# A Fourier mixer and its feed-forward block on one core: the inverse step of the next token group moved into another unit, with store, split and weight-sum steps rescheduled

## The chip, the cores and the metric

The kernel runs on one core of a Trainium2 chip. The metric is the device time of one execution in microseconds; the change is judged by the median of several runs. A core has TensorE (PE; its weight loads are PEld), VectorE (DVE), ScalarE (ACT), GpSimd (POOL) and SyncE (SP), which here only issues DMAs. Each engine works through its own queue in order.

## The reference, cut to what matters

```python
X = np.fft.rfft(x, axis=1)                     # x: (8, 3008, 256)
Y = X * (filt_r + 1j * filt_i)[None]
y = np.fft.irfft(Y, n=3008, axis=1).reshape(8 * 3008, 256)
h = y @ w_in                                   # (24064, 256) @ (256, 2048)
g = h - np.tanh(h)
out = g @ w_out                                # (24064, 2048) @ (2048, 256)
```

Eight sequences of 3008 tokens are filtered in the frequency domain and then go through two matrix products with `h - tanh(h)` between them. All is float32.

## The kernel before, in words

**Work.** 3008 = 64 x 47, so the transform is made in steps: a 64-point step on the input (`first` for batches 1 and 2, `split_first` for batches 3 to 7, a program of its own for batch 0), written to a DRAM buffer `ct1`; a 47-point step, the filter and the 47-point step back (`middle`), from `ct1` to a DRAM buffer `ct2`; and an inverse 64-point step (`last`), from `ct2` to on-chip tiles `ut` and `tu`, which are the input of the first matrix product. Tokens are treated in 48 groups: 8 batches `p` of 6 groups `c`.

**Units.** For each group the feed-forward block runs in four units `u`, each a quarter of the 2048 inner columns. Unit `U = 4 * group + u`. In the loop over `U`, three units overlap: the first product of unit U (`up`), the nonlinearity of U - 1 (`shrink`), the second product of U - 2 (`down`). Both products take seven block products for eight, with sums of blocks (`combine` for the data, `sums` for the weights). So a unit has 7 + 7 block products of two 128x128 by 128x256 pieces each; each piece shows as two matmuls in the trace, 56 in a unit. The first group, whose weight sums are not there yet, uses plain products (`up_plain`, `down_plain`).

**Slots.** `up` is written out by hand. Between its products it calls `d` and `e` (the next piece of `down`), `s` (the next piece of `shrink`) and five slots `t(0)` to `t(4)`. A slot first puts up to four entries of the list `outs` on SyncE's queue (`store_some(4)`), in slot 2 makes the output tile of the group before and adds its 32 (or 48) stores to `outs` (`store`), and then runs at most one piece of side work: the inverse step of the next group at (u, k) = (3, 2); a piece of `first`; a piece of `split_first` at the places `SPLIT_AT`, each (c, u, k); or a piece of `middle` (a plan of `there`, eight filter pieces and `back`, four times a batch; `there` stands at (2, 0)). Side work puts its writes to `ct1` and `ct2` at the front of `outs`.

**Order on the engines.** The order in which the program calls these is the order on each engine's queue. In `up`, bank `x` takes product 1, then in turn 6, 7 and 4 on top, with ScalarE (`s1`, `u2`, `u3`, L629) or VectorE (L671) reading it between; bank `y` takes product 2 (read by L646); bank `z` takes product 5 (L663), then 3 on top (L679). The accumulators of `down` are the banks `o0` to `o3`; `o3` is read last, by L834. Bank `t` is left over for side work, which borrows others when they are free.

**Side work.** `last` (L582) makes two banks with 64x64 matmuls; ScalarE copies one out (L586), VectorE adds and subtracts the other (L589, L590), GpSimd makes the four sums `tu` (L603 to L606). `packed` (L402) makes the 47-point steps with 24x32 matmuls in four banks. `split_first` (L341) makes the 64-point step with 32x32 matmuls in four banks, in three parts a batch: load of `f` (L314) and of two x tiles (L321, L325, L327), their sum (L332) and difference (L334), matmuls and copies (L346, L347), sums and differences (L349, L350) and writes to `ct1`. At unit 3 of a batch's last group the loop begins `split_first` of batch p + 3, whose first loads are issued there, and `middle` of batch p + 2 (loads of `a2`, L375, and `ft`, L383). The sum L332 stands in slot (0, 0, 2) of the next batch.

Of the kernel before, what the change touches and what calls it, by code (L numbers as in the profile page):

```python
# [9 lines left out]
F32 = mybir.dt.float32  # L10
# [7 lines left out]
BATCH, SEQ, DM = 8, 3008, 256  # L18
# [6 lines left out]
CH = 4  # L25
# [92 lines left out]
def kernel(  # L118
# [104 lines left out]

        return jobs

    def sums(u):

        w = (wu if u < 4 else wd)[:, :, 256 * (u % 4):256 * (u % 4) + 256]
        V.tensor_add(w[:, 4], w[:, 6], w[:, 3])
        yield  # L230
        for to, one_in, less in ((5, 4, 0), (2, 1, 5), (6, 0, 6)):
            V.tensor_sub(w[:, to], w[:, one_in], w[:, less])
            yield

    def begun(tiles, job, queue=nc.sync):
        j = converted(tiles, *job, queue)
# [70 lines left out]
    def split_first(b, z):  # L307

        quarters = [slice(32 * k, 32 * k + 32) for k in range(4)]
        for c, tags in enumerate((("t", "o1", "y", "o0"), ("t", "o3", "o1", "o2"),  # L310
                                  ("t", "o1", "y", "o0"))):
            f = tr.tile([128, XH, 128], F32, tag="f", bufs=2, name="f")[:, 0:2]
            f = f.rearrange("p a (b n) -> p (a b) n", n=32)
            nc.sync.dma_start(f, split_d[:, 256 * c:256 * c + 256])  # L314
            x0, x1 = (tr.tile([128, XH, DM], F32, tag="x", bufs=2, name="x_sb") for _ in range(2))
            for h, t in enumerate((x0, x1)):
                at = b * SEQ + 32 * h * NR
                for g in range(2):
                    r = 2 * FH * c + FH * g
                    low, high = quarters[g], quarters[2 + g]  # L320
                    nc.sync.dma_start(t[low], dram(x.tensor, (at + r) * DM,  # L321
                                                   [[NR * DM, 32], [1, FH * DM]]))
                    lo = int(r == 0)
                    if lo:
                        nc.sync.dma_start(t[high, 0], dram(x.tensor, at * DM,  # L325
                                                           [[NR * DM, 32], [1, DM]]))
                    nc.sync.dma_start(t[high, lo:FH], dram(x.tensor, (at + NR - r - lo) * DM,  # L327
                                                           [[NR * DM, 32], [-DM, FH - lo], [1, DM]]))
            yield
            both = tr.tile([128, 2, 2, DM], F32, tag="a1", bufs=1, name="a1")  # L330
            even = both.rearrange("p v n c -> p (v n) c")
            V.tensor_add(even, x0, x1)  # L332
            yield
            V.tensor_sub(x1, x0, x1)  # L334
            yield
            banks = z(tags)
            for n in range(2):
                for k, (bank, part) in enumerate(zip(banks, quarters)):
                    for j, to in enumerate(quarters):
                        m, odd = 2 * (j // 2) + n, j % 2  # L340
                        nc.tensor.matmul(bank[to, n], f[part, 2 * m + odd],  # L341
                                         (x1 if odd else even)[part, m], start=True, stop=True)
            made = both, x0.rearrange("p (v n) c -> p v n c", v=2)
            other = x1[:, 0:2]
            for g, a1 in enumerate(made):
                ACT.copy(a1[:, 1], banks[2 + g])  # L346
            ACT.copy(other, banks[1])  # L347
            for g, a1 in enumerate(made):
                V.tensor_add(a1[:, 0], other if g else banks[0], a1[:, 1])  # L349
                V.tensor_sub(a1[:, 1], other if g else banks[0], a1[:, 1])  # L350
                outs[:0] = [(dram(ct1[b], ((1 - j % 2) * NH + 2 * FH * c + FH * g +
                                           2 * (j // 2)) * DM,
                                  [[2 * NH * DM, 32], [64 * NH * DM, 2], [1, 2 * DM]]),
                             a1[part].rearrange("p v n c -> p v (n c)"))
                            for j, part in enumerate(quarters)]
                yield

    SPLIT_AT = {(0, 0, 2), (0, 1, 0), (0, 1, 3), (1, 1, 1), (1, 1, 4), (2, 0, 2),
                (3, 0, 2), (4, 2, 0), (4, 2, 2), (4, 3, 0), (5, 0, 2), (5, 1, 0), (5, 1, 3),
                (5, 2, 2)}  # L360

    def parts(t, b, g, first_block=0, n=4, step=1):

# [24 lines left out]
    def packed(banks, o, weight, data):  # L388

        ahead, whole, late = [], [], []  # L390
        for q, bank in enumerate(banks):
            part = slice(PAD * q, PAD * q + NH)
            for col in range(4):
                to, at = bank[PAD * col:PAD * col + PAD], data(q, col)[part]
                plain, special = (wide[part, weight(q, col, last)] for last in (0, 1))
                if o == 3 and 3 == (col if weight is WAYS[0] else q):
                    ahead.append((to[:, 0], plain, at[:, 0:DM]))
                    late.append((to[:, 1], special, at[:, DM:2 * DM]))
                else:
                    whole.append((to.rearrange("p n c -> p (n c)"), plain, at))  # L400
        for to, weights_of, at in ahead + whole + late:
            nc.tensor.matmul(to, weights_of, at, start=True, stop=True)  # L402
# [165 lines left out]

    e2s, uts = {}, {}

    def last(i, z):

        b, c = groups[i]
        n = sum(widths(c))
# [3 lines left out]
        for h in range(2):  # L578
            for j, r in enumerate(order(c)):
                for bank, half in zip(banks, rows):  # L580
                    for m, part in enumerate(rows):
                        nc.tensor.matmul(bank[part, h, j],  # L582
                                         e2[half, r - CH * c, h * 128 + 64 * m:h * 128 + 64 * m + 64],
                                         gt[half, r - CH * c], start=True, stop=True)
        odd = tr.tile([128, 2, CH, 64], F32, tag="e1", bufs=2, name="odd")
        ACT.copy(odd, banks[1])  # L586
        u4 = ut.rearrange("p h (j n) -> p h j n", n=128)
        m = sum(w == 128 for w in widths(c))
        V.tensor_add(u4[:, :, :, 0:64], banks[0], odd)  # L589
        V.tensor_sub(u4[:, :, 0:m, 127:63:-1], banks[0][:, :, 0:m], odd[:, :, 0:m])  # L590
        w = n // 2
        if i == 0:
            uts[i] = (ut, None, w)
# [13 lines left out]

    hs, gs = {}, {}

    def up(U, d, e, s, t):  # L610

        i, u = divmod(U, 4)
        b, tu, w = uts[i]
        rhs = [b[0][0], b[1][0], b[1][1], tu[:, 3, 0:w], tu[:, 0, 0:w], tu[:, 1, 0:w],
               tu[:, 2, 0:w]]
# [24 lines left out]
        mm(X, 1, True)  # L640
        mm(Y, 2, True)
        s1 = copied("s1")
        t(0)
        d()
        shrinks(0)
        V.tensor_add(h[:, 0, :, 0:w], Y, s1)  # L646
# [359 lines left out]
    with tc.tile_pool(name="tr", bufs=2) as tr, tc.manual_schedule():  # L1006
# [278 lines left out]
        with tc.tile_pool(name="dn", bufs=2) as dn, \  # L1285
# [5 lines left out]
            def zd2(name, shape):  # L1291
                return [ps.tile(shape, F32, tag=tag, bufs=1, name=name) for tag in "ty"]

            def zd4(tags):
                return [ps.tile([128, 2, DM], F32, tag=tag, bufs=1, name="pm") for tag in tags]

# [55 lines left out]
            kinds.update({at: "filter" for at in FILTERED})  # L1352

            firsts, mids = {2: fs}, {}
            for U in range(total + 2):
                i, u = divmod(U, 4)
                if U == 6:
                    assert not pending
                    late = (None for u in (3, 5, 6, 7) for _ in sums(u))
                if U == 3:  # L1360
                    G.dma_start(mats[:, 0:10 * PAD], wide_d[0:KM])
                if U < total:
                    p, c = groups[i]
                    if c == 0 and u == 0 and 0 < p < BATCH - 1:
                        plan += STAGES
                    if u == 0 and i + 1 < len(groups) and c + 1 < NC:
                        e2s[i + 1] = load_e2(*groups[i + 1])
                    if u == 2 and i + 1 < len(groups) and c + 1 == NC:
                        assert not plan
                        e2s[i + 1] = load_e2(*groups[i + 1])  # L1370
                    if u == 3 and c + 1 == NC and p + 3 < BATCH:
                        firsts[p + 3] = split_first(p + 3, zd4)
                        next(firsts[p + 3])
                    if u == 3 and c + 1 == NC and p + 2 < BATCH:
                        mids[p + 2] = middle(p + 2, zd4)
                        next(mids[p + 2])
# [15 lines left out]
                def e():  # L1392

                    next(dw, None)
                    converting((U < 6) * (3 if U > 1 else 1))

                def s():

# [2 lines left out]
                def t(k):  # L1401
# [7 lines left out]
                    if i == 1 and pos == LEAD - 7:  # L1409
# [1 line left out]
                        mids[1] = middle(1, zd4)  # L1411
                        next(mids[1])
                        plan.extend(STAGES)
                    if (u, k) == (3, 2) and i + 1 < len(groups):
                        next(last(i + 1, z2))
                    elif due and due[0] <= pos and (U < 4 or u < 3 and k == 2):
                        due.pop(0)
                        next(firsts[2])
                    elif (c, u, k) in SPLIT_AT and 0 < p < BATCH - 2:
                        next(firsts[p + 2])  # L1420
                    elif plan and plan[0] == kinds.get((u, k)):
                        plan.pop(0)
                        next(mids[p + 1])
# [58 lines left out]
```

## Time and profile before

| | |
|---|---|
| median of three runs | 2556.81 us (2555.12 to 2558.86) |
| the profiled execution's own time | 2556.91 us |
| span of its trace | 2555.1 us |
| TensorE, weight loads | 2534.3 us, 2169.1 us busy |
| VectorE, ScalarE, GpSimd | 1873.3 us, 1667.7 us, 1481.2 us busy |

The span is the time from the first to the last instruction in the trace. Busy time is the time in which an engine had at least one instruction under way; issuing a DMA does not count. Rows of the timeline give start, duration (of all instructions that the row merges), engine, line, and `out<-in` with shapes; the count is at the end, and in brackets the idle time of the engine before it with what ended it.

### The profile page before, as it was taken

The numbers are of one execution on the slowest core, as the hardware profiler recorded it, in microseconds if no ns is written. First come the engines' busy times: TensorE is split into PE (matmuls) and PEld (weight loads), VectorE is DVE, ScalarE is ACT, GpSimd is POOL, SyncE is SP. The second block draws the span as 40 slices with busy tenths as digits, with TensorE's granted clock in tenths as the row PEclk, the third lists the DMA queues.
The fourth block names the chain that finished last, engine by engine and source line by source line (L and its number), as shares of the span: only waits on it lengthen the run. The fifth ranks groups of instructions, "written<-read, shape, count | busy, mean of one in ns | idle before, by whom it ended". The sixth has DMA issues, their size and how long they took to land.

```text
span 2555.1 us, 44617 instructions
## 1 busy us (share of the span) xinstructions
PE 2534.3 (99%) x17072; PEld 2169.1 (85%) x17072; DVE 1873.3 (73%) x2262; ACT 1667.7 (65%) x2499; POOL 1481.2 (58%) x1120
## 2 busy tenths in 40 slices
PE   9999999999999999999999999999999999999998
PEld 8578889888898888988888888888889888898887
DVE  6887776887678876888668886688866877555555
ACT  4556666666666666666666666666666666666665
POOL 5266665666466665666556665566645666555552
PEclk9999999999999999999999999999999999999999
DMA  8863224422343323342233322443123322110110
GB/s 247 263 173 103 65 53 109 102 65 61 81 104 91 81 59 98 80 110 58 73 95 98 84 65 61 107 101 97 36 67 85 93 66 51 26 32 18 25 22 19
DMA packets 334240, 212.42 MB, mean 83 GB/s; under 512 B 231709, under 2 KB 305595, under 8 KB 330369
## 3 DMA queue, kind: packets, MB, share of 16 engines
q1 hardware_dynamic: 319667, 185.98, 29.6%
q0 software_dynamic: 11120, 16.16, 2.4%
q10 hardware_dynamic: 3230, 7.34, 0.8%
q8 instruction: 136, 2.23, 0.4%
q14 instruction: 87, 0.71, 0.1%
HBM read 128.86 MB, written 83.39 MB: 83 GB/s over the span
## 4 chain that ended last, share of the span: by engine, by line
PE 94%; DVE 2%; DMA 2%; issue 0%; ACT 0%; POOL 0%; SPq 0%; ACTq 0%; POOLq 0%; DVEq 0%
PE o L795 44%; PE x L623 25%; PE z L623 12%; PE y L623 6%; PE pm L402 3%; PE pu L582 2%; PE pm L341 1%; DMA ct<-a 1%; DMA x<-in_x_dram 1%; DMA filt<-in_filt_r_dram 0%; DMA ct<-e 0%; DVE h L745 0%; PE pf L298 0%; PE o L857 0%; PE pe L1115 0%
## 5 line engine op out<-in xcount | busy, mean ns | idle before, releaser
L795 PE MATMUL o<-t,wd 128*128 128x256 f32 (+1 forms) x3008 | 763.2, 376 | 0.0
L603 POOL TENSOR_TENSOR t<-h 128x512 f32<-128x512 f32 (+1 forms) x186 | 305.5, 1643 | 712.6 <-DVE h L745 696.0
L745 DVE TENSOR_TENSOR h<-h,y 128x1024 f32<-128x1024 f32 (+1 forms) x384 | 579.3, 1509 | 161.9 <-ACT y L741 158.5
L795 PEld LDWEIGHTS o<-t,wd 128*128 128x128 f32 x3008 | 568.3, 190 | 86.3 <-POOL o L827 15.1
L623 PE MATMUL x<-tu,wu 128*128 128x256 f32 (+1 forms) x2256 | 576.0, 378 | 0.6 <-ACT u L629 0.6
L795 PE MATMUL o<-h,wd 128*128 128x256 f32 (+1 forms) x2256 | 573.2, 377 | 0.2 <-DVE h L745 0.2
L795 PEld LDWEIGHTS o<-h,wd 128*128 128x128 f32 x2256 | 425.3, 190 | 71.7 <-issue 18.4
L629 ACT COPY s<-x 128x512 f32<-128x512 f32 (+1 forms) x188 | 108.8, 578 | 564.9 <-PE x L623 564.5
L623 PEld LDWEIGHTS x<-tu,wu 128*128 128x128 f32 x2256 | 422.9, 190 | 58.3 <-issue 3.7
L738 ACT ACTIVATE y<-y 128x1024 f32<-128x1024 f32 (+1 forms) x384 | 399.4, 1040 | 12.0
L741 ACT ACTIVATE y<-y 128x1024 f32<-128x1024 f32 (+1 forms) x384 | 399.8, 1041 | 4.6
L735 ACT ACTIVATE y<-h 128x1024 f32<-128x1024 f32 (+1 forms) x384 | 400.5, 1043 | 2.5 <-DVE h L671 1.7
L604 POOL TENSOR_TENSOR t<-h,t 128x512 f32<-128x512 f32 (+1 forms) x186 | 314.0, 1688 | 14.6
L606 POOL TENSOR_TENSOR t<-h,t 128x512 f32<-128x512 f32 (+1 forms) x186 | 304.6, 1638 | 0.0
L605 POOL TENSOR_TENSOR t<-h 128x512 f32<-128x512 f32 (+1 forms) x186 | 289.8, 1558 | 0.0
L629 ACT COPY u<-x 128x512 f32<-128x512 f32 (+1 forms) x376 | 213.6, 568 | 56.8 <-PE x L623 53.6
L671 DVE COPY h<-x 128x512 f32<-128x512 f32 (+1 forms) x188 | 127.7, 679 | 127.1 <-PE x L623 127.0
L623 PE MATMUL z<-tu,wu 128*128 128x256 f32 (+1 forms) x752 | 190.1, 375 | 0.4 <-DVE h L679 0.4
L623 PE MATMUL z<-ut,wu 128*128 128x256 f32 (+1 forms) x752 | 190.1, 375 | 0.4 <-DVE h L663 0.4
L623 PE MATMUL x<-ut,wu 128*128 128x256 f32 (+1 forms) x752 | 190.1, 375 | 0.2 <-DVE h L671 0.2
L623 PE MATMUL y<-ut,wu 128*128 128x256 f32 (+1 forms) x752 | 190.1, 375 | 0.2 <-ACT a L300 0.2
L663 DVE TENSOR_TENSOR h<-z,u 128x512 f32<-128x512 f32 (+1 forms) x188 | 127.1, 676 | 73.0 <-ACT u L629 72.1
(211 smaller groups left out, 2798.1 us busy)
## 6 DMA issues: line engine op xcount, KB each, us to landing
ft<-filt SPq DMA_DIRECT2D x28, 1024.0 KB
ct<-nn SPq DMA_DIRECT2D x56, 512.0 KB
e<-ct SPq DMA_DIRECT2D x47, 512.0 KB
a<-ct SPq DMA_DIRECT2D x112, 192.0 KB
out_dram<-ot SPq DMA_DIRECT2D x1248, 16.0 KB
x_sb<-in_x_dram SPq DMA_DIRECT2D x110, 128.0 KB
ct<-a SPq DMA_DIRECT2D x60, 128.0 KB
ct<-x_sb SPq DMA_DIRECT2D x60, 128.0 KB
```

The source lines that it names most:

```text
L603: by.tensor_sub(t[0], b[0][1], b[0][0])
L604: by.tensor_sub(t[1], b[1][1], t[0])
L605: by.tensor_sub(t[2], b[1][1], b[0][1])
L606: by.tensor_sub(t[3], b[1][0], t[1])
L623: nc.tensor.matmul(bank[:, k], wu[:, q - 1, (2 * u + k) * 128:(2 * u + k + 1) * 128], rhs[q - 1], start=(first and k == 0), stop=True, ski ...
L629: ACT.copy(t, X)
L671: V.tensor_copy(h[:, 2, :, 0:w], X)
L735: ACT.activation(y[k], ht[k], AF.Arctan, scale=TURN)
L738: ACT.activation(y[k], y[k], AF.Tanh, scale=BEND)
L741: ACT.activation(y[k], y[k], AF.Square, scale=SCALE, accum_out=y_sums[:, 2 * U + k // 2:2 * U + k // 2 + 1])
L745: V.tensor_mul(ht[k], ht[k], y[k])
L795: nc.tensor.matmul(product(q), wd[:, q - 1, (2 * u + k) * 128: (2 * u + k + 1) * 128], rhs[q - 1][:, k], start=(u == 0 and k == 0 and q == ...
```

## The change

- `last` of the next group moves from slot (3, 2) to slot (2, 0) in the groups for which `merged` holds: those where `there` or a split part stands in that slot. It then uses banks `y` and `x`, and ScalarE copies both out (`held`). In these units `up` calls slot 0 ahead of its first product instead of behind its second. The load of `e2` in a batch's last group moves from unit 2 to unit 0.
- `packed` takes its four banks in the order 0, 2, 3, 1 on the way there.
- `split_first`: ScalarE copies all four banks instead of three, each of the four sums and differences gets a slot, and the parts use other banks; `SPLIT_AT` has 23 places instead of 14. The third part's matmuls move from (5, 1, 3) to (5, 2, 0), its last difference from (5, 2, 2) to (5, 2, 4).
- At unit 3 of a batch's last group, all of `outs` is put on SyncE's queue before the loads of `split_first` and `middle`.
- Of the weight sums of four quarters, which ran two a slot from unit 6, the first three of each run in unit 5 (three at each `e`), and the last of each in unit 6.

```diff
-    def sums(u):
+    def sums(u, n=4):
 
         w = (wu if u < 4 else wd)[:, :, 256 * (u % 4):256 * (u % 4) + 256]
         V.tensor_add(w[:, 4], w[:, 6], w[:, 3])
         yield
-        for to, one_in, less in ((5, 4, 0), (2, 1, 5), (6, 0, 6)):
+        for to, one_in, less in ((5, 4, 0), (2, 1, 5), (6, 0, 6))[:n - 1]:
             V.tensor_sub(w[:, to], w[:, one_in], w[:, less])
             yield
+
+    def last_sum(u):
+
+        w = (wu if u < 4 else wd)[:, :, 256 * (u % 4):256 * (u % 4) + 256]
+        V.tensor_sub(w[:, 6], w[:, 0], w[:, 6])
...
-        for c, tags in enumerate((("t", "o1", "y", "o0"), ("t", "o3", "o1", "o2"),
-                                  ("t", "o1", "y", "o0"))):
+        for c, tags in enumerate((("t", "y", "o1", "o0"), ("t", "o3", "o1", "o2"),
+                                  ("t", "o3", "o1", "o2"))):
...
-            other = x1[:, 0:2]
+            others = x1.rearrange("p (v n) c -> p v n c", v=2)
+            for k in (1, 0, 2, 3):
+                ACT.copy(made[k - 2][:, 1] if k > 1 else others[:, k], banks[k])
+            yield
             for g, a1 in enumerate(made):
-                ACT.copy(a1[:, 1], banks[2 + g])
-            ACT.copy(other, banks[1])
-            for g, a1 in enumerate(made):
-                V.tensor_add(a1[:, 0], other if g else banks[0], a1[:, 1])
-                V.tensor_sub(a1[:, 1], other if g else banks[0], a1[:, 1])
+                V.tensor_add(a1[:, 0], others[:, g], a1[:, 1])
+                yield
+                V.tensor_sub(a1[:, 1], others[:, g], a1[:, 1])
...
-    SPLIT_AT = {(0, 0, 2), (0, 1, 0), (0, 1, 3), (1, 1, 1), (1, 1, 4), (2, 0, 2),
-                (3, 0, 2), (4, 2, 0), (4, 2, 2), (4, 3, 0), (5, 0, 2), (5, 1, 0), (5, 1, 3),
-                (5, 2, 2)}
+    SPLIT_AT = {(0, 0, 2), (0, 1, 0), (0, 1, 3), (1, 0, 1), (1, 0, 2), (1, 1, 1), (1, 1, 2),
+                (1, 1, 4), (2, 0, 2), (3, 0, 2), (4, 2, 0), (4, 2, 1), (4, 2, 2), (4, 2, 3),
+                (4, 2, 4), (4, 3, 0), (5, 0, 2), (5, 1, 0), (5, 2, 0), (5, 2, 1), (5, 2, 2),
+                (5, 2, 3), (5, 2, 4)}
...
-        for q, bank in enumerate(banks):
+        for q in (0, 2, 3, 1) if weight is WAYS[0] else range(4):
+            bank = banks[q]
...
-        odd = tr.tile([128, 2, CH, 64], F32, tag="e1", bufs=2, name="odd")
-        ACT.copy(odd, banks[1])
+        even, odd = banks
+        for k in (1, 0) if held else (1,):
+            t = tr.tile([128, 2, CH, 64], F32, tag="e1", bufs=2, name=("even", "odd")[k])
+            ACT.copy(t, banks[k])
+            even, odd = (even, t) if k else (t, odd)
...
-        V.tensor_add(u4[:, :, :, 0:64], banks[0], odd)
-        V.tensor_sub(u4[:, :, 0:m, 127:63:-1], banks[0][:, :, 0:m], odd[:, :, 0:m])
+        V.tensor_add(u4[:, :, :, 0:64], even, odd)
+        V.tensor_sub(u4[:, :, 0:m, 127:63:-1], even[:, :, 0:m], odd[:, :, 0:m])
...
+    def merged(U):
+
+        i, u = divmod(U, 4)
+        b, c = groups[i]
+        return u == 2 and (1 < c < NC - 1 if b == 0 else
+                           c < (4 if b == BATCH - 2 else NC) and b < BATCH - 1)
+
     def up(U, d, e, s, t):
 
         i, u = divmod(U, 4)
+        if merged(U):
+            t(0)
...
         s1 = copied("s1")
-        t(0)
+        if not merged(U):
+            t(0)
...
+            def z2u(name, shape):
+                return [ps.tile(shape, F32, tag=tag, bufs=1, name=name) for tag in "yx"]
...
+            extra = (None for u in (3, 5, 6, 7) for _ in sums(u, 3))
...
-                    late = (None for u in (3, 5, 6, 7) for _ in sums(u))
+                    for _ in extra:
+                        pass
+                    late = (last_sum(u) for u in (3, 5, 6, 7))
...
-                    if u == 0 and i + 1 < len(groups) and c + 1 < NC:
+                    at = (2, 0) if merged(4 * i + 2) else (3, 2)
+                    if i + 1 < len(groups) and u == (2 if (p, c) == (0, NC - 1) else 0):
+                        assert c + 1 < NC or not plan
                         e2s[i + 1] = load_e2(*groups[i + 1])
-                    if u == 2 and i + 1 < len(groups) and c + 1 == NC:
-                        assert not plan
-                        e2s[i + 1] = load_e2(*groups[i + 1])
+                    if u == 3 and c + 1 == NC:
+                        store_some(len(outs))
...
+                    if U == 5:
+                        assert not pending
+                        for _ in range(3):
+                            next(extra, None)
...
-                    if (u, k) == (3, 2) and i + 1 < len(groups):
-                        next(last(i + 1, z2))
+                    behind = i + 1 < len(groups) and (u, k) == at
+                    if behind:
+                        next(last(i + 1, z2 if u == 3 else z2u, u == 2))
+                    if behind and u == 3:
+                        pass
                     elif due and due[0] <= pos and (U < 4 or u < 3 and k == 2):
```

More of the change, by code (lines that the diff above doesn't have):

```diff
@@ L569, with last @@
     e2s, uts = {}, {}
-    def last(i, z):
+    def last(i, z, held=False):
         b, c = groups[i]
```

## Prediction

> **What bounds the kernel now.** I read the page first (busy times and the chain that ended last), then the groups of TensorE instructions with shapes kept apart, and then the timeline around the places that the diff touches.
>
> ```profile
> span 2555.1 us, 44617 instructions
> PE 2534.3 (99%) x17072; PEld 2169.1 (85%) x17072; DVE 1873.3 (73%) x2262; ACT 1667.7 (65%) x2499; POOL 1481.2 (58%) x1120
> PE 94%; DVE 2%; DMA 2%; issue 0%; ACT 0%; POOL 0%; SPq 0%; ACTq 0%; POOLq 0%; DVEq 0%
> ```
>
> TensorE is busy for 2534.3 of 2555.1 us, and 94% of the chain is its own. The diff takes no matmul away, so it can win only the 21 us of idle time and whatever is lost between matmuls; against that, every microsecond for which it makes TensorE wait counts in full. I therefore look at the distance between starts of matmuls.
>
> ```profile
> L795 PE MATMUL o<-t,wd 128*128 128x256 f32 x2560 | 659.5, 380 | 0.0
> L582 PE MATMUL pu<-gt,e 64*64 64x64 f32 x3072 | 56.4, 221 | 2.4 <-DMA e<-ct 1.1 <-DVE h L646 0.8 <-issue 0.4
> L402 PE MATMUL pm<-a,mats_sb 24*32 24x512 f32 x840 | 34.4, 599 | 0.0
> ```
>
> One matmul takes 0.38, 0.22 and 0.60 us in these three forms. The next rows are an inverse step that stands alone (L582), with the products ahead of it and behind it, and what drains it:
>
> ```profile
> 1207.50 1.89 PE L795 MATMUL o<-h,wd 128*128 128x256 f32 x8
> ...
> 1212.25 0.59 PE L795 MATMUL o<-t,wd 128*128 128x256 f32 x2
> ...
> 1212.77 1.16 PE L582 MATMUL pu<-gt,e 64*64 64x64 f32 x64
> ...
> 1213.87 1.13 PE L623 MATMUL x<-tu,wu 128*128 128x256 f32 x4
> 1214.00 0.59 ACT L586 COPY odd<-pu 128x512 f32<-128x512 f32 x1 [0.83 <-PE pu L582]
> ...
> 1214.62 0.69 DVE L589 TENSOR_TENSOR ut<-pu,odd 128x512 f32<-128x512 f32 x1 [0.76 <-ACT odd L586]
> ...
> 1215.99 0.73 POOL L603 TENSOR_TENSOR tu<-ut 128x256 f32<-128x256 f32 x1 [1.00 <-DVE ut L590]
> ```
>
> Eight products in 1.89 us are one each (1.89 - 0.38) / 7 = 0.216 us. The last product ahead of the step starts at 1212.25 + 0.59 - 0.38 = 1212.46, and the step 0.31 later: 0.09 over the normal 0.216. The last of the 64 starts at 1212.77 + 1.16 - 0.22 = 1213.71, and the product behind it 0.16 later, where 64 columns at the same rate would need 0.05: again 0.1. So going into the 64-row form and coming out of it costs 0.09 to 0.1 us each way.
>
> **The change part by part.** *The joined inverse step.* The forward step of the filter (L402) shows the same two prices:
>
> ```profile
> 472.88 1.03 PE L623 MATMUL y<-ut,wu 128*128 128x256 f32 x4
> 473.83 1.22 PE L402 MATMUL pm<-a,mats_sb 24*32 24x512 f32 x32
> 474.98 0.48 PE L795 MATMUL o<-h,wd 128*128 128x256 f32 x1
> ```
>
> It enters 473.83 - (472.88 + 1.03 - 0.38) = 0.30 us after the product ahead of it, 0.09 over 0.216, and leaves 0.53 us after its last start (474.45), 0.1 over the 0.43 that 512 columns need. Two separate visits pay four switches. Joined, 64-row and then 32-row, they pay three if the switch between the two small forms costs the same, and two if it is free; no row shows that switch, so its price lies between 0 and 0.1, and I take the 0.09 of the nearest rows. The Trainium skill, TensorEngine Tiling (Array Packing), section Key Properties, says that changing the tiling mode drains the engine while tiles of one mode run independently. By that the sum is the one that I take, and the rows agree with it for both small forms. `merged` holds for 3 groups of batch 0, 6 each of batches 1 to 5, and 4 of batch 6: 37 of 47. Gain 37 x 0.09 = **3.4 us** (6.8 if free).
>
> What moves with it: one more ScalarE copy (0.59), two VectorE sums (0.69 each) and four GpSimd operations (0.73 each), all from unit 3 to unit 2. The step now uses banks x and y, and the unit's first product X waits until ScalarE has emptied x. The old copy began at 1214.00 and ended 0.88 us after the last L582 start; X now comes 0.15 + 0.6 + 0.5 = 1.2 us after that start, since the L402 visit stands between. This holds if ScalarE is free:
>
> ```profile
> 473.08 0.59 ACT L629 COPY s<-x 128x512 f32<-128x512 f32 x1 [1.66 <-PE x L623]
> ```
>
> ScalarE has been idle for 1.66 us here, a place where the new copy would stand; so I cost the wait at nothing. Y has another 0.86 us. VectorE's room in a unit 2:
>
> ```profile
> 145.40:159.20 13.80, 13.80 (x53) 9.90 (x54) 6.23 (x8) 9.46 (x14) 0.84 (x3) 1.00 0.98 281
> 174.30:190.20 15.90, 14.23 (x121) 11.60 (x121) 15.83 (x20) 8.57 (x12) 13.93 (x13) 1.00 0.23 45
> 884.40:897.90 13.50, 13.50 (x98) 11.16 (x96) 10.60 (x15) 8.84 (x13) 5.72 (x5) 1.00 0.38 86
> ```
>
> (Length, then busy time of PE, PEld, DVE, ACT, POOL.) In the third row, a unit 2, VectorE has 10.6 of 13.5 us; with 1.4 more in a unit 1.2 longer it still fits. GpSimd has 5.7, and 2.9 more fits. Both cost nothing.
>
> *Filter and split steps.* In the first group of batches 1 to 5 the forward step waits for bank o3, which VectorE reads late:
>
> ```profile
> 425.37 0.42 DVE L834 TENSOR_TENSOR o<-o,p 128x256 f32<-128x256 f32 x1
> ...
> 425.59 1.47 PE L402 MATMUL pm<-a,mats_sb 24*32 24x512 f32 x32
> ```
>
> 1.47 against 1.22 us. With o3 taken last and the split's sums (two of 0.69 right before) spread over later slots, this goes: 5 x 0.25 = **1.2 us**. ScalarE's extra copy per split falls into slots where it waits for matmuls; I cost it at nothing, at most its 0.59 x 15 = 9 us if nothing covered it.
>
> *Weight sums.* The third window above is typical; the second is unit 7, where VectorE is full (15.83 of 15.90). There TensorE waits for it:
>
> ```profile
> PE pu L582 <- DVE h L646: 0.8, 1, 0.8
> PE z L623 <- DVE h L679: 0.4, 1, 0.4
> PE z L623 <- DVE h L663: 0.4, 1, 0.4
> ```
>
> Twelve of the sixteen sums go to unit 5, which has 6.23 of 13.80 busy (first row), and none stays in unit 7. Gain **1.6 us**; what could be late next is unit 5, which has 7 us to spare.
>
> *The emptied store list.* This is the part that I think decides. Ahead of the split step's and filter's loads at unit 3 of a batch's last group, all pending stores are now put on SyncE's queue. Before:
>
> ```profile
> 1000.45 1.74 SPq L911 DMA_DIRECT2D ct<-x_sb  x4
> 1002.23 1.88 SPq L911 DMA_DIRECT2D out_dram<-ot  x4
> 1004.15 0.43 SPq L314 DMA_DIRECT2D f<-f_split  x1
> ...
> 1009.63 0.43 SPq L327 DMA_DIRECT2D x_sb<-in_x_dram  x1
> 1010.10 1.71 SPq L375 DMA_DIRECT2D a<-ct  x4
> ...
> 1012.27 15.75 SPq L911 DMA_DIRECT2D out_dram<-ot  x20
> ...
> 1029.02 2.32 SPq L911 DMA_DIRECT2D out_dram<-ot  x5
> ```
> ```profile
> 1001.53 1.22 DVE L745 TENSOR_TENSOR h<-h,y 128x1024 f32<-128x1024 f32 x1
> 1002.67 0.68 DVE L679 TENSOR_TENSOR h<-z,u 128x512 f32<-128x512 f32 x1
> ...
> 1022.09 1.21 DVE L332 TENSOR_TENSOR a<-x_sb 128x1024 f32<-128x1024 f32 x1
> 1023.43 0.62 DVE L663 TENSOR_TENSOR h<-z,u 128x448 f32<-128x448 f32 x1
> ```
> ```profile
> 1015.43 0.92 PE L623 MATMUL x<-ut,wu 128*128 128x224 f32 x4
> ...
> 1026.02 0.92 PE L623 MATMUL z<-ut,wu 128*128 128x224 f32 x4
> ```
>
> The three fences are SyncE's queue, VectorE and TensorE. Unit 3 began 56 products of 0.216 and an inverse step of 1.2 ahead of 1015.43, at 1002.1. In the code, a store list of 32 is made in slot 2 of unit 2, slots 3 and 4 each issue four entries (now four ct1 writes and four stores), and four ct1 writes of the last split difference go in front: 32 stand there at unit 3, 4 ct1 writes and 28 stores. From unit 3's first product: the last difference, now in slot 4, stands between L745 and L679 on VectorE, behind one more 0.69 sum: 1002.67 + 2 x 0.69 - 1002.1 = 2.0 us. Four ct1 writes: 1.8. 28 stores at (2.32 - 0.43) / 4 = 0.47: 13.2. The load of f and ten of x: 1004.15 to 1010.06, 5.9. Landing of the last: no row of its own; between 0 and 5 us, taken as 1.5. Sum **24.4 us**. Needed: unit 3 is now 12.1 long, and L332, which adds two x tiles, stood 1022.09 - 1015.43 = 6.7 behind the next unit's start: 18.8. VectorE, which works in order, would wait 5.6 us at L332. Behind L332 is L663, whose end (1024.05) releases Z at 1026.02: 2.0 us of cover. TensorE then waits **3.6 us**. This happens at the ends of batches 1 to 4 (a split load follows, and its last difference is that late). At batch 0 24 stores go, with no ct1 write and unit 3 of old length: 11.4 + 5.9 + 1.5 = 18.8 against 13.4 + 6.7 = 20.1, no loss. 4 x 3.6 = **14.4 us**. Ends: with the difference done at 0.3, 0.43 a store and a landing of 0, the loads are there at 20.0 and cost nothing; with 0.79 a store (the 20 in 15.75, which stood behind large loads) and a landing of 5 they would cost 16 us each; the five in 2.32 are nearer, as nothing large is under way ahead of the flush. The earlier e load (unit 0 instead of 2 in the last group) goes by an almost empty queue and costs nothing; the next one, behind the late a and ft loads, has some 4 us left.
>
> Sum: 2556.9 (the profiled execution's own time, 0.1 over the median of the runs) - 3.4 - 1.2 - 1.6 + 14.4 = **2565.1 us**.
>
> **The rivals.** *The loads are in time* (stores issue faster or the difference is done earlier than I think): only the gains stay, 2556.9 - 6.2 = 2550.7 us, or 2547.3 with a free switch between small forms. For it: each of my five terms is an estimate, and 4 us a boundary less is enough. It decides at a last x landing 20.8 us after unit 3 begins. Against it: 28 stores alone are 12 us at the fastest rate seen.
>
> *ScalarE is busy when bank x is to be emptied.* If one activation stood ahead of the copy,
>
> ```profile
> 476.11 1.07 ACT L735 ACTIVATE y<-h 128x1024 f32<-128x1024 f32 x1
> ```
>
> X would wait 0.88 + 1.07 - 1.2 = 0.75 us, 37 times: 28 us on top of the gains alone, 2578 us. Against it stands the 1.66 us of idle time above.
>
> *The clock falls in the new gaps.* The first matmuls of the program are slow:
>
> ```profile
> L1055 PE MATMUL warm<-filt 120*128 120x256 f32 x30 | 8.4, 449 | 1.5 <-DVE filt L1144 1.5
> ```
>
> 449 ns against 380 on average for 30. If TensorE ran at half rate for as long as it had idled, 3.6 us, each of the four gaps would cost 1.8 more: 2572.3 us. No gap behind the start is as long, so the trace can't say. The Trainium skill, TensorE: Matmul & The Clock Gate, Part 1, says that an idle window of some 3.4 us throttles the clock to half; by that rule the gaps lie just at the edge.
>
> **How the numbers follow.** Forecast 0.55 (its own range 2560 to 2572, from 2.3 to 5.3 us a boundary); loads in time 0.25; ScalarE 0.07; clock 0.08; loads only a little late, so that loss and gain cancel, 0.05. A measurement of this kernel can tell about 0.2%, 5.1 us, from no change. Slower by more than that: four fifths of the forecast (0.44), ScalarE and clock, 0.59. Within: the rest of the forecast, the cancelling case and a tenth of the second, 0.18. Faster: 0.23. The range 2547 to 2576 leaves out ScalarE and the tails, some 0.15.
>
> **What would show it.** Right: in the changed profile SyncE issues 32 writes in a row ahead of f_split, the add of x tiles on VectorE waits for DMA, and TensorE's wait on h L663's line at Z appears four times, 3 to 4 us each; L582 and L402 stand together, 37 times, 0.15 us between them; unit 7's waits are gone. Wrong: no DMA wait at that add, or a wait of X on ScalarE behind each joined visit.

## The result, and the profile after

| | before | changed |
|---|---|---|
| median | 2556.53 us (2555.12 to 2558.86, 4 runs) | 2570.86 us (2570.37 to 2575.17, 4 runs) |
| the profiled execution | 2556.91 us, span 2555.1 | 2570.37 us, span 2568.6 |

The ratio is 1.0059, with an interval of 1.0046 to 1.0071: slower by 0.6%, where 2565.1 us was forecast. In the changed kernel L590 is the inverse step (L582 before), L410 the 47-point step (L402), L684 the sum that frees bank z (L663), L337 the sum of the x tiles (L332), L932 the stores (L911), L643 and L816 the two products.

The page of the changed kernel:

```profile
span 2568.6 us, 44556 instructions
PE 2535.2 (99%) x17072; PEld 2181.5 (85%) x17072; DVE 1931.4 (75%) x2262; ACT 1693.5 (66%) x2551; POOL 1543.3 (60%) x1120
PE 91%; DMA 3%; SPq 2%; DVE 1%; POOL 1%; issue 1%; ACT 1%; DVEq 0%; ACTq 0%; POOLq 0%
```

TensorE's busy time is nearly the same, but the chain of work now runs 3% of the span through DMA and 2% through SyncE's queue. TensorE's waits (total, times, longest):

```profile
PE z L643 <- DVE h L684: 14.9, 4, 4.4
PE pu L590 <- DMA e<-ct: 1.8, 1, 1.8
PE o L816 <- POOL t L614: 1.5, 1, 1.5
```

The first is the forecast's: bank z, four times, 14.9 us against 14.4. The timelines of SyncE, VectorE and TensorE at the end of batch 2 show the chain of it:

```profile
1004.84 1.73 SPq L932 DMA_DIRECT2D ct<-x_sb  x4
1006.61 13.26 SPq L932 DMA_DIRECT2D out_dram<-ot  x28
1019.91 0.44 SPq L319 DMA_DIRECT2D f<-f_split  x1
...
1024.62 1.41 SPq L332 DMA_DIRECT2D x_sb<-in_x_dram  x1
```
```profile
1020.14 1.87 DVE L766 TENSOR_TENSOR h<-h,y 128x1024 f32<-128x1024 f32 x1 [2.31 <-ACT y L762]
1028.17 1.23 DVE L337 TENSOR_TENSOR a<-x_sb 128x1024 f32<-128x1024 f32 x1 [6.16 <-DMA x_sb<-in_x_dram]
1029.32 0.62 DVE L684 TENSOR_TENSOR h<-z,u 128x448 f32<-128x448 f32 x1
```
```profile
1025.11 1.03 PE L816 MATMUL o<-t,wd 128*128 128x256 f32 x4
1029.99 1.86 PE L643 MATMUL z<-ut,wu 128*128 128x224 f32 x4 [3.85 <-DVE h L684]
1031.64 1.70 PE L643 MATMUL x<-ut,wu 128*128 128x224 f32 x4
```

Read downward: 28 stores hold the queue for 13.26 us, the last x load has been issued at 1026.03, its data are there 2.1 us later, VectorE has waited 6.16 us at the sum of the x tiles, and behind that sum stands the one that frees z. Four matmuls of the next product then take 1.70 us, where such a group took 0.92 before. The windows say why; the column after the five engines is the granted TensorE clock:

```profile
1014.00:1030.00 16.00, 12.15 (x61) 10.90 (x59) 6.62 (x8) 7.71 (x11) 5.02 (x4) 0.97 0.48 119
1030.00:1036.00 6.00, 6.00 (x16) 5.36 (x17) 4.42 (x5) 2.33 (x3) 4.18 (x3) 0.52 1.04 263
1036.00:1042.00 6.00, 6.00 (x32) 5.54 (x31) 2.26 (x4) 4.68 (x9) 1.67 (x2) 1.00 0.19 74
```

Sixteen matmuls in six microseconds at a clock of 0.52, then 32 in six at 1.00: in the six microseconds behind the gap half the work is done. This was the rival with a chance of 0.08, and it came on top of the forecast. In this trace's record of the clock the four stretches at half rate behind the gaps are 3.41, 6.83, 6.83 and 3.41 us long, 20.5 us together; TensorE was busy for 18.8 us of them, and half of that, 9.4 us, was lost.

A joined visit in TensorE's timeline (a visit is a run of small-form matmuls between two products; here an inverse step and a filter step):

```profile
832.31 1.03 PE L643 MATMUL z<-ut,wu 128*128 128x256 f32 x4
833.27 1.16 PE L590 MATMUL pu<-gt,e 64*64 64x64 f32 x64
834.36 1.16 PE L410 MATMUL pm<-a,mats_sb 24*32 24x512 f32 x32
835.45 1.13 PE L643 MATMUL x<-ut,wu 128*128 128x256 f32 x4
836.41 1.03 PE L643 MATMUL y<-ut,wu 128*128 128x256 f32 x4
```

Between the last L590 start (833.27 + 1.16 - 0.22 = 834.21) and L410 lie 0.15 us, so the switch between the two small forms does cost its 0.1. The row behind the visit has 1.13 us for four matmuls where others have 1.03: the second matmul behind a visit starts 0.10 us late. The prediction quoted such a row of before (1213.87, 1.13) and missed this. Of the 37 joined visits 27 go on with a filter step, as here, and 10 with a split step.

### The profile page after: what moved, and what is told of

It reads as the page before. It is cut to its first block, busy times and chain, and to the rows that moved or that the text cites. A ratio compares the mean times of both kernels' runs of the same rounds, so it can differ in the third digit from the quotient of the medians.

```text
span 2568.6 us, 44556 instructions
## 1 busy us (share of the span) xinstructions
PE 2535.2 (99%) x17072; PEld 2181.5 (85%) x17072; DVE 1931.4 (75%) x2262; ACT 1693.5 (66%) x2551; POOL 1543.3 (60%) x1120
## 4 chain that ended last, share of the span: by engine, by line
PE 91%; DMA 3%; SPq 2%; DVE 1%; POOL 1%; issue 1%; ACT 1%; DVEq 0%; ACTq 0%; POOLq 0%
PE o L816 42%; PE x L643 24%; PE z L643 12%; PE y L643 6%; PE pm L410 2%; PE pu L590 2%; SPq L932 1%; PE pm L346 1%; DMA filt<-in_filt_r_dram 1%; DMA x<-in_x_dram 0%; DMA x_sb<-in_x_dram 0%; DMA ct<-e 0%; PE pf L303 0%; DMA filt<-zero 0%; DMA ct<-a 0%
## 5 line engine op out<-in xcount | busy, mean ns | idle before, releaser
L816 PE MATMUL o<-t,wd 128*128 128x256 f32 (+1 forms) x3008 | 762.7, 376 | 1.5 <-POOL t L614 1.5
L614 POOL TENSOR_TENSOR t<-h 128x512 f32<-128x512 f32 (+1 forms) x186 | 308.3, 1658 | 721.5 <-DVE h L766 654.9
L766 DVE TENSOR_TENSOR h<-h,y 128x1024 f32<-128x1024 f32 (+1 forms) x384 | 571.8, 1489 | 157.5 <-ACT y L762 157.5
L816 PEld LDWEIGHTS o<-t,wd 128*128 128x128 f32 x3008 | 568.7, 190 | 86.4 <-POOL o L848 15.1
L643 PE MATMUL x<-tu,wu 128*128 128x256 f32 (+1 forms) x2256 | 571.5, 376 | 0.1
L816 PE MATMUL o<-h,wd 128*128 128x256 f32 (+1 forms) x2256 | 571.2, 376 | 0.2 <-DVE h L766 0.2
L643 PEld LDWEIGHTS x<-tu,wu 128*128 128x128 f32 x2256 | 427.3, 190 | 54.3 <-issue 3.7
L816 PEld LDWEIGHTS o<-h,wd 128*128 128x128 f32 x2256 | 429.6, 191 | 51.4 <-issue 0.8
L617 POOL TENSOR_TENSOR t<-h,t 128x512 f32<-128x512 f32 (+1 forms) x186 | 338.5, 1820 | 0.0
L615 POOL TENSOR_TENSOR t<-h,t 128x512 f32<-128x512 f32 (+1 forms) x186 | 314.0, 1688 | 14.6
L616 POOL TENSOR_TENSOR t<-h 128x512 f32<-128x512 f32 (+1 forms) x186 | 280.5, 1508 | 0.0
L643 PE MATMUL z<-ut,wu 128*128 128x256 f32 (+1 forms) x752 | 193.3, 380 | 14.9 <-DVE h L684 14.9
L643 PE MATMUL x<-ut,wu 128*128 128x256 f32 (+1 forms) x752 | 197.1, 385 | 0.6 <-DVE h L692 0.6
L684 DVE TENSOR_TENSOR h<-z,u 128x512 f32<-128x512 f32 (+1 forms) x188 | 127.3, 677 | 90.7 <-ACT u L649 90.4
L643 PE MATMUL y<-ut,wu 128*128 128x256 f32 (+1 forms) x752 | 192.6, 379 | 0.5 <-ACT a L305 0.5
L643 PE MATMUL z<-tu,wu 128*128 128x256 f32 (+1 forms) x752 | 190.0, 375 | 0.0
```

The source lines that it names most:

```text
L614: by.tensor_sub(t[0], b[0][1], b[0][0])
L615: by.tensor_sub(t[1], b[1][1], t[0])
L616: by.tensor_sub(t[2], b[1][1], b[0][1])
L617: by.tensor_sub(t[3], b[1][0], t[1])
L643: nc.tensor.matmul(bank[:, k], wu[:, q - 1, (2 * u + k) * 128:(2 * u + k + 1) * 128], rhs[q - 1], start=(first and k == 0), stop=True, ski ...
L766: V.tensor_mul(ht[k], ht[k], y[k])
```

## The experiments

The theory after the result: the four gaps come from the stores ahead of the loads, the clock falls because TensorE idles in them, and all the rest of the change is a gain. Rivals: the later split difference and the shorter unit 3 make the loads late by themselves; the flush costs its length wherever it stands; the slow matmuls have another cause than idling; the joins bring nothing.

**Only the front of the list ahead of the loads.**

```diff
-                        store_some(len(outs))
+                        store_some(4)
```

> The changed kernel, but at unit 3 of a batch's last group only the four entries at the front of the store list (the last split difference's ct1 writes) go ahead of the loads, not all 32. Theory: the 28 output stores ahead of the loads, 13.3 us on SyncE's queue, are what makes the add of the x tiles late; then its wait of 6.2 us, TensorE's four waits at Z (14.9 us) and the slow matmuls behind them (about 9.6 us beyond the waits) all go: 2570.9 - 25 = 2546 us, below the kernel before. Rival: the late difference and the shorter unit 3 make the loads late by themselves; then most of the four waits stays and the time is above 2560 us.

Measured: 2544.4 us, ratio to before 0.9947 (0.9933 to 0.996). The waits at z are gone, and VectorE finds the x tiles there:

```profile
1000.44 1.74 SPq L932 DMA_DIRECT2D ct<-x_sb  x4
1002.22 0.44 SPq L319 DMA_DIRECT2D f<-f_split  x1
```
```profile
1015.75 1.87 DVE L766 TENSOR_TENSOR h<-h,y 128x1024 f32<-128x1024 f32 x1 [2.31 <-ACT y L762]
1017.54 1.21 DVE L337 TENSOR_TENSOR a<-x_sb 128x1024 f32<-128x1024 f32 x1
```

Without the stores ahead of the loads the whole loss is gone; the four entries that stay ahead are the ct1 writes that the filter step reads. The first rival falls: the late difference and the shorter unit 3 don't make the loads late by themselves.

**The flush in the kernel before.**

```diff
+                    if u == 3 and c + 1 == NC:
+                        store_some(len(outs))
```

> The kernel before, with only one line of the change: the whole store list is put on SyncE's queue at unit 3 of a batch's last group. Theory: 24 stores go ahead of the loads, 11.4 us; the last x tile is there some 23.5 us into the time scale in which the add stood at 22.1 and had 2.0 us of cover, so VectorE waits 1 to 1.5 us and TensorE not at all: 2556.5 us, within 2 us. The flush alone would then not have been enough; the later difference and the shorter unit 3 used up the rest. Rival: the flush costs its whole length wherever it stands: 2570 us or more.

Measured: 2564.5 us, ratio 1.0029 (1.0019 to 1.0039). Neither number was right. Four of the waits at z are boundaries, of 1.38 to 1.85 us:

```profile
1005.98 15.71 SPq L911 DMA_DIRECT2D out_dram<-ot  x32
1021.74 0.43 SPq L314 DMA_DIRECT2D f<-f_split  x1
```
```profile
1029.77 1.22 DVE L332 TENSOR_TENSOR a<-x_sb 128x1024 f32<-128x1024 f32 x1 [3.86 <-DMA x_sb<-in_x_dram]
```

The expectation had counted 24 stores in the flush; the row has 32, four of slot 4 and 28. With 4 x 0.47 us more, the same reckoning makes VectorE some 3 us late (3.86 in the row), less 2.0 us of cover: 1 to 1.4. The remaining 2 us of each gap in the changed kernel are put down to the shorter unit 3 (1.2 us) and the later difference; no run takes these two apart. So it is neither harmless alone, as the theory had it, nor does it cost its length wherever it stands: it costs 1.4 to 1.9 us a boundary alone, and the rest of the change makes that twice as much.

**A flush of 28 entries.**

```diff
-                        store_some(len(outs))
+                        store_some(28)
```

> The changed kernel, but at most 28 entries go ahead of the loads (24 stores and 4 ct1 writes), which takes 1.9 us off each of the four gaps of 3.4 to 4.5 us; 1.5 to 2.6 us stay. If the TensorE clock falls only behind a gap of more than some 3.4 us, nothing runs at half rate any more: 2546 + 8 = 2554 us and a granted clock of 0.999. If what follows a gap is lost in proportion to the gap (9.6 us beyond 15.6 us of waits in the changed kernel): 2546 + 8 x 1.6 = 2559 us.

Measured: 2555.3 us, ratio 0.9993 (0.9982 to 1.0004): no difference from before can be told, since gain and loss cancel. The gaps are shorter, and the clock fell behind one of the four. Here are the four products behind the gaps, from TensorE's timeline, and two windows behind the third and the fourth:

```profile
718.50 0.83 PE L643 MATMUL z<-ut,wu 128*128 128x224 f32 x3 [1.69 <-DVE h L684]
...
1025.84 1.02 PE L643 MATMUL z<-ut,wu 128*128 128x224 f32 x4 [1.04 <-DVE h L684]
...
1333.90 1.02 PE L643 MATMUL z<-ut,wu 128*128 128x224 f32 x4 [1.78 <-DVE h L684]
...
1642.47 1.86 PE L643 MATMUL z<-ut,wu 128*128 128x224 f32 x4 [2.27 <-DVE h L684]
```
```profile
1334.00:1337.40 3.40, 3.40 (x18) 3.27 (x19) 3.40 (x4) 1.65 (x3) 1.67 (x2) 1.00 1.08 197
1642.40:1645.80 3.40, 3.33 (x9) 3.04 (x10) 3.11 (x5) 0.00 (x0) 1.50 (x2) 0.51 1.10 151
```

Behind 1.78 us the clock stays at 1.00; behind 2.27 it is 0.51. So the slow matmuls come wholly or not at all and not in proportion to the gap, and a gap of 3.4 us isn't needed. But the length of a gap alone doesn't decide either. Near the start of the program TensorE waits once for the load of an inverse step, 1.63 us in the first experiment's kernel and 2.54 us in the run with the weight sums moved back; under each row stands a window, the first behind its gap, the second around the end of it, with the granted clock:

```profile
75.84 0.33 PE L590 MATMUL pu<-gt,e 64*64 64x64 f32 x4 [1.63 <-DMA e<-ct]
77.02:80.43 3.41, 3.41 (x45) 2.77 (x35) 1.70 (x4) 1.16 (x2) 0.00 (x0) 0.50 0.99 238
```
```profile
77.51 0.33 PE L590 MATMUL pu<-gt,e 64*64 64x64 f32 x4 [2.54 <-DMA e<-ct]
76.56:79.98 3.42, 2.16 (x68) 1.91 (x69) 0.88 (x2) 0.60 (x2) 0.00 (x0) 1.00 0.74 216
```

The shorter gap is followed by half rate, the longer one is not (the clock stays at 1.00 behind this window too). What tells them apart in the traces is a grid: within a run the clock changes only at times that are whole multiples of 3.413 us apart (in the changed kernel 76.62, 718.33, 1028.94, 1342.97 and 1656.99 us). The 1.63 us, with smaller gaps, made 1.91 us of idle time within one such stretch; the 2.54 us fell on two, with 1.59 and 1.26 us of idle time.

In all eleven traces, leaving out the first 10 and the last 17 us, each of the twelve stretches at full rate with 1.85 us or more of idle time was followed by half rate; of those at full rate with less, up to 1.78 us, all but two were not (1.62 us in the run with block sums on VectorE, and 0.71 us in the run with the step first; why is open).

**The gaps filled.**

```diff
         t(4)
+        if u == 0 and 12 <= i <= 30 and i % 6 == 0:
+            fill = ps.tile([128, 2, 256], F32, tag="t", bufs=1, name="fill")
+            for _ in range(7):
+                nc.tensor.matmul(fill[:, 0], wu[:, 0, 0:128], wu[:, 0, 0:256],
+                                 start=True, stop=True)
         mm(Z, 3, False)
```

> The changed kernel, with 14 extra matmuls (7 products into the idle bank t, 3.0 us, results unused) just ahead of the product at Z where it waits, at the starts of batches 2 to 5. They lie inside the gaps of 3.2 to 4.4 us, so no more than 1.4 us of each stays idle. If the half-rate matmuls behind the gaps come from TensorE having idled, they go: 2571 - 9.6 = 2561 us, with the waits of the add on VectorE unchanged. If they come from something else (the transfers, VectorE's late sums), the time stays at 2571 us and matmuls behind the gaps still take twice as long.

Measured: 2561.0 us, ratio 1.0024 (1.0014 to 1.0034), where the changed kernel has 1.0059. TensorE at the end of batch 2, and the window behind the gap:

```profile
1023.35 3.19 PE L702 MATMUL fill<-wu 128*128 128x256 f32 x14
1026.82 1.02 PE L643 MATMUL z<-ut,wu 128*128 128x224 f32 x4 [0.29 <-DVE h L684]
1027.68 0.92 PE L643 MATMUL x<-ut,wu 128*128 128x224 f32 x4
```
```profile
1027.00:1033.00 6.00, 6.00 (x31) 5.74 (x32) 5.37 (x7) 4.16 (x8) 4.34 (x3) 1.00 1.04 261
```

VectorE still waits 5.62 us for the x tiles (6.16 in the changed kernel), the transfers and VectorE's sums behind it are the same, and the clock is at 1.00, here and behind the other three gaps. So it is idling that lowers it, and beside the 14.9 us of waits the four boundaries cost about 9 us of slow matmuls (0.35% of 2557, the difference of the two ratios; 9.4 us by the clock's record).

**The joins undone.**

```diff
     def merged(U):
-        i, u = divmod(U, 4)
-        b, c = groups[i]
-        return u == 2 and (...)
+        return False
```

(On top of the four entries of the first experiment, as all that follow.)

> As e1_front_only, with the join undone as well: the inverse step stands at (3, 2) in every group, in banks t and y, and slot 0 comes behind the second product again. The difference to e1_front_only is what the 37 joins are worth. By the switches of the prediction alone: 37 x 0.09 = 3.4 us, 2549.5 us. With the 0.10 us that the second matmul behind every visit to a small form was late in the traces as well (one visit less each): 37 x 0.2 = 7 us or a little more, 2553 us. If the join brings nothing by itself: 2546 us.

Measured: 2560.9 us, ratio 1.002 (1.0011 to 1.0029): 16.5 us above the kernel with joins, more than each theory said. A new wait explains part:

```profile
PE x L640 <- ACT u L646: 5.9, 11, 0.5
```

Ten of the eleven, 0.53 us each, stand in a unit 2 with a split step: ScalarE works there without a break from the split's four copies to a copy of x (`u2` or `u3`) that TensorE's next product waits for. The eleventh, of 0.5 us, stands near the start of the program, as one of 0.6 does in the kernel before, so the new waits are 5.3 us. In the joined form none of the ten is in the trace; there the split's matmuls come ahead of the unit's first product and not behind its second. The rest, some 11 us, is put down to the join itself; the rows of the traces, reckoned below, give 9.6.

**The step first, the inverse step behind it.**

```diff
-                    if behind:
-                        next(last(i + 1, z2 if u == 3 else z2u, u == 2))
...
                         next(mids[p + 1])
+                    if behind and u == 2:
+                        next(last(i + 1, z2u, True))
```

> As e1_front_only, but in the joined slot the filter or split step is issued first and the inverse step behind it. The number of visits is the same; what changes is that nothing stands between the inverse step and the unit's first product, which needs bank x emptied by ScalarE. Theory: the cover of 1.2 us was needed. X then waits 0.88 - 0.15 = 0.7 us behind a filter step (27 times) and some 2 us behind a split step, whose four copies stand ahead on ScalarE (10 times): 2544 + 19 + 20 = 2583 us, with waits of X on ScalarE in the trace. If ScalarE were quick enough without the cover: 2544 us.

Measured: 2608.1 us, ratio 1.0203 (1.0187 to 1.0219), 64 us above the other order. The two waits that are of the order:

```profile
PE x L643 <- ACT odd L596: 34.3, 37, 1.5
PE pm L410 <- DVE o L855: 2.5, 6, 0.4
```

All 37 joined visits now make X wait for ScalarE, 0.7 us behind a filter step and 1.5 behind a split step, 34.3 us in all where the theory had 39. Some 26 us more, which the theory did not have, stand inside the filter and split steps. For one filter step, whose 32 matmuls take 1.16 us in the first experiment's kernel, TensorE's rows and one of VectorE's are:

```profile
845.16 2.10 PE L410 MATMUL pm<-a,mats_sb 24*32 24x512 f32 x32
845.72 0.42 DVE L855 TENSOR_TENSOR o<-o,p 128x256 f32<-128x256 f32 x1
846.19 0.15 PEld L410 LDWEIGHTS pm<-a,mats_sb 24*32 24x32 f32 x8 [0.83 <-DVE o L855]
```

Its last eight matmuls wait for an accumulator bank that VectorE reads until 846.14. With the inverse step ahead, that read is over in time (in the first experiment's kernel it ends at 829.85, and the step begins at 829.96). So the order of the join gives cover twice, to the bank of the step and to bank x: the same work, turned round, costs about four times what undoing the join costs.

**The weight sums back in units 6 and 7.**

```diff
-            extra = (None for u in (3, 5, 6, 7) for _ in sums(u, 3))
+            extra = iter(())
...
-                    late = (last_sum(u) for u in (3, 5, 6, 7))
+                    late = (None for u in (3, 5, 6, 7) for _ in sums(u))
```

> As e1_front_only, with the sixteen weight sums of four quarters back in units 6 and 7, two a slot. One look: the start of the program varies by 2 us from run to run, so the trace decides. If moving the sums removed the waits of unit 7, they are back (inverse step on h L646's line 0.8 us, z twice 0.4), and the wait of 1.5 us on GpSimd at 195 us, which all kernels with the moved sums show, is gone, since TensorE gets there later: net about 1 us. If that wait on GpSimd has nothing to do with the sums, it stays.

Measured: 2543.5 us in a single run. The waits between 170 and 200 us:

```profile
PE pu L590 <- DVE h L667: 0.8, 1, 0.8
PE z L643 <- DVE h L700: 0.4, 1, 0.4
PE z L643 <- DVE h L684: 0.4, 1, 0.4
```

They are back, and the wait on GpSimd is gone: 1.6 us for 1.5. Moving the sums gains nothing in this stretch, because the next engine in line is as late.

**Block sums of one group on VectorE.**

```diff
-        combine(b, [...], V if pending else G)
+        combine(b, [...], V if pending or i == 2 else G)
```

> As e1_front_only, with the four block sums of the third group's inverse step (0.7 to 1.8 us each on GpSimd, behind five filter DMAs that GpSimd issues) made by VectorE. If they are what keeps GpSimd from the sums that TensorE waits for at 195 us, that wait of 1.5 us goes: 2543 us, and nothing else moves. If it was the DMA issues alone, it stays at about 2544 us.

Measured: 2543.5 us, ratio 0.9953 (0.9939 to 0.9966). In this stretch the trace shows no wait of TensorE any more, so these four sums kept GpSimd. The ratio can't tell 1.5 us from none (the kernel without it has 0.9947). This and the first experiment's kernel are the two, of those run several times, that beat both, by half a per cent against before.

**The bank order as before.**

```diff
-        for q in (0, 2, 3, 1) if weight is WAYS[0] else range(4):
+        for q in range(4):
```

> As e1_front_only, with the forward filter step's four banks in the old order 0, 1, 2, 3. One look; the trace decides, by the joined visits' lengths between 240 and 2490 us. If the new order is what took the o3 wait of 0.25 us off the first group's step in batches 1 to 5, at least 5 x 0.25 = 1.2 us come back in the five such joined visits, and more where the joined visit starts its filter part earlier behind L834's read. If the later sums of the split step alone had done it, those five visits stay as they are.

Measured: 2547.1 us in a single run beside 2557.3 of before. The filter part of the joined visit in batch 3's first group, in this kernel and then with the new order:

```profile
1037.38 1.22 PE L410 MATMUL pm<-a,mats_sb 24*32 24x512 f32 x32
```
```profile
1036.48 1.16 PE L410 MATMUL pm<-a,mats_sb 24*32 24x512 f32 x32
```

0.06 us, in five such visits 0.3 us. The 0.25 us that this step waited for o3 before didn't come back with the old order, so the order is worth nearly nothing. The join, whose inverse step now stands ahead, could have hidden the wait; but in the run without joins the last read of o3 ends at 1039.11, where the same step begins at 1040.86, while in the kernel before the split's two sums stood ahead of that read and it ended at 1041.54, behind the step's start at 1041.34. So the split's later sums are enough.

## Why the prediction was right, and where not

- **The emptied list: right, and to the size.** Its five terms against the trace, from unit 3's first product at 1003.30: difference done 1.5 us in (2.0 said), four ct1 writes 1.8 (1.8), 28 stores 13.3 (13.2), f and x loads 6.1 (5.9), landing 2.1 (1.5, which the prediction took from no row). VectorE waited 6.16 us (5.6), TensorE 3.2 to 4.4 (3.6), four times, and not at batch 0. Removing the stores removed all of it.
- **The clock: the rival should have been part of the forecast.** It had a chance of 0.08 and is what the sum lacked most. Its price per gap was said as 1.8 us, half rate for as long as TensorE had idled, and came as some 2.3: the half-rate stretches were 3.41 or 6.83 us long, whatever the gap. The rule of the Trainium skill that stood beside it (TensorE: Matmul & The Clock Gate, Part 1: an idle window of some 3.4 us throttles to half) names the state that the traces show. They don't agree that the whole window has to be idle: 1.85 us out of 3.41 was enough, and a gap of 2.27 us.
- **The join: right in kind, too small.** Said 3.4 us. From the rows: the two visits took 1.41 and 1.45 us with 0.10 behind each, less two normal distances of 0.216: 2.63. Joined, 835.45 - (832.31 + 1.03 - 0.38) + 0.10 - 0.216 = 2.37. That is 0.26 each, 37 x 0.26 = 9.6 us. The switch between the small forms costs the same as the others, as the forecast took it, and the one saved is its 0.09; 0.10 is the second matmul behind a visit, and the rest a short wait inside the step (1.22 to 1.16) that the inverse step now hides.
- **The cover of bank x: right.** No wait of X on ScalarE stands in the changed kernel behind a joined visit; turned round, X waits at all 37.
- **Split and filter: right in sum (1.2 us), wrong in cause.** The wait went with the later sums, and the order was not needed. ScalarE's extra copy was costed at nothing, and so it is, but only under the join: without it ten waits of 0.53 us appear behind the copies.
- **Weight sums: wrong.** The 1.6 us are gone and 1.5 come back as a wait on GpSimd. "What could be late next is unit 5" looked at the unit that got the work and not at the engine behind the one that was relieved.

The sum by the rows: 2556.9 + 14.9 of waits + about 9 of clock - 9.6 - 1.2 - 0.1 = 2570 us, where 2570.4 was measured in the profiled execution. The forecast was 5 us low: the clock (9 us) and the weight sums (1.5) were left out, and the join (6.2 too little) nearly made up for them. That it came so near is in part luck, and the range of 2547 to 2576 us, which reaches from faster to slower, would have held much else. What bears the prediction out is the wait at z: its place, its cause and its 14.9 us against 14.4.

## What to carry to other kernels

When a list of pending transfers is emptied ahead of a load, count its entries and multiply by the queue's issue time: here 28 stores of 16 KB were 13 us, and only the four ct1 writes had to go ahead. When a wait is taken from the bound engine, look at which engine is next in line and not at the one that took over the work. A gap on TensorE should be priced with the slow matmuls behind it (here some 2.3 us for each of 3.2 to 4.4), and a join of two steps by the copy that the next product waits for and by the bank that the step itself waits for.

## What the runs showed of the hardware

- Within a run the granted clock changed only at times that are whole multiples of 3.413 us apart, and fell to 0.50 for 3.41 or 6.83 us (the end of the program left out). All twelve stretches of this grid at full rate in which TensorE idled for 1.85 us or more were followed by half rate; of those with up to 1.78 us all but two were not. The length of one gap doesn't tell: the clock fell behind one of 1.63 us and stayed behind one of 2.54 us that lay across two stretches.
- The second matmul behind a visit to 64-row or 32-row matmuls starts 0.10 us late (1.13 us for four instead of 1.03), beyond the 0.1 us of going in and coming out.
